# The first 500 steps of all engines in a listed order, and the first feed-forward unit in two halves

## The chip, the cores and the metric

The kernel runs on one core of one Trainium2 chip. The metric is the device time of one execution in microseconds, as the median of several runs.

The engines are named as in the profile: PE (TensorE; PEld are its weight loads), DVE (VectorE), ACT (ScalarE), POOL (GpSimd) and SP (SyncE, which issues nearly all DMAs).

## The reference

Two blocks follow one another. The first is a linear attention with decay, over 4 batches, 8 heads, 768 positions and 64 columns per head, in blocks of 64 positions:

```python
for b in range(nb):
    intra = np.einsum('bhic,bhjc->bhij', qb, kb) * Dmask[None]
    intra = np.einsum('bhij,bhjd->bhid', intra, vb)
    inter = np.einsum('bhid,bhde->bhie', qb * lam_pow[None], kv_state)
    out[:, :, sl] = intra + inter
    kb_dec = kb * rev_pow[None]
    kv_state = lam_block[None, :, None, None] * kv_state + np.einsum('bhsd,bhse->bhde', kb_dec, vb)
```

Its result, as 3072 rows of 512, goes through a feed-forward block with a leaky ReLU:

```python
h = x @ w_in                  # 512 x 2048, stored as 64-bit floats
g = np.maximum(0.01 * h, h)
out = (g @ w_out)             # 2048 x 512, stored as 64-bit floats
```

## The kernel before, in words

**Tiles.** The 3072 rows are 24 chunks of 128 rows (two blocks of 64); six chunks make a batch, and four chunks make a group `g` of 512 rows, six groups in all. The 2048 columns of `w_in` are eight pieces `p` of 256 columns. Group by piece is a *unit*, written (g,p): `up(g, p)` multiplies the group's 512 rows by the piece, applies the leaky ReLU and stores the result G in DRAM; `down` reads it back for the second product.

**Three products for one.** Operands are split into a high part h and a low part l, with a mixed part m of both, so that a unit has three products (h, l, m) for each of two halves `f` of the piece's columns. A product is four matmuls with 512 columns, one after the other into one PSUM bank (L640). After h and l ACT scales the bank in place (L658); after m ACT applies the ReLU into `gs` (L661), and SP stores `gs` (L664).

**A chunk of attention.** SP loads k and q (L338, two DMAs each) and v (L388). `transposes(c)` turns k and q on PE (L403), k into a bank and q into `pt`; ACT copies them out (L414, L415); k is scaled by the decay (L419) and q by its powers (L423). `scores(c)` multiplies q and k into the lower half of `psc` and k and v into the state's increments in its upper half (L313, 32 small matmuls each). DVE masks the scores (L452) and adds the increments to the state (L457, L459), with POOL multiplying the state by the decay in between (L462). `outputs(c)` sums masked scores by v and state by q into `po` (L313: 40 or 48 small matmuls, then, after a tiny read of `po` by DVE or ACT (L491), 8 or 16 more). ACT and DVE split the result into xh (L507), xl (L508) and xm (L510), the rows of the units' right-hand side.

**A piece of weights.** `w_in(p)` loads two halves of 512 KB into one of three buffers `raw` (L566), assembles 32-bit floats from the 64-bit words with three ACT steps (L578, L580, L582) and two DVE steps (L584, L585) per half, and splits them into wh (L591 on ACT or L593 on DVE), wl (L596) and wm (L602).

**Order.** The engines' instructions are not scheduled by the framework. Every step is given to a `Plan` by `add`, with the engines that may run it, its estimated length, what it reads and writes, and a rank from its place in the list `seq`. `emit` then simulates the engines with these lengths and the handover times `LAG`, always takes the step that can start first (by rank where several can), and issues the instructions in that order. Each engine runs its own steps strictly in order and waits by semaphores. `begin` and `end` bind a round's PE steps into a chain. Where the planned PE waits over 0.4 us before the first unit, `emit` puts in fillers: transposes of the identity without use (L266); nine more stand at the very start.

`seq` opens with chunks 0 to 3 one by one (`alone`), weight 1, chunk 4's start (`begun`), round 4, unit (0,1), weight 0, round 5, weights 2 and 3, units (0,0), (0,2), (0,3), round 6, and then unit (1,1) in two pieces of 384 and 128 rows, around round 7, weight 4, unit (0,4) and weight 7.

**Banks and buffers.** The units' banks are b10 and b2 for the first two, then b10, b11, b2 in turn. Transposes of k for chunks 0 to 3 use b11, those of q use `pt`. k, q and v of a chunk lie in one of two places by the chunk's parity.

Of the kernel before, what the change touches and what calls it, by code (L numbers as in the profile page):

```python
# [35 lines left out]

class Plan:
# [5 lines left out]
    SOON = dict(LAG, DMA=2.0)  # L43

    def __init__(self):
        self.ops, self.last, self.rank = [], {}, 0.0
        self.chain, self.chains = None, {}
        self.warm, self.slack, self.more = 0.0, 0.0, {}
        self.first = {"PE": 0.0, "ACT": 0.0, "DVE": 3.4, "POOL": 0.0, "DMA": 0.2}
        self.cold, self.idle, self.spare = 6.0, None, None  # L50
# [10 lines left out]
    def add(self, eng, us, fn, reads=(), writes=(), rank=0.0):  # L61

        n, deps = len(self.ops), set()
        for k in reads:
            w, r = self.last.setdefault(k, [None, []])
            if w is not None:
                deps.add(w)
            r.append(n)
        for k in writes:
            w, r = self.last.setdefault(k, [None, []])  # L70
            if w is not None:
                deps.add(w)
            deps.update(r)
            self.last[k] = [n, []]
        deps.discard(n)
        ways = {eng: us} if isinstance(eng, str) else dict(zip(eng, us))
        if self.slack:
            self.more[n] = self.slack
        if self.chain is not None:
            self.chains[self.chain].append(n)  # L80
        self.ops.append((ways, fn, deps, (self.rank + rank, n), set(writes)))

    def emit(self):
        n = len(self.ops)
        follows, heads = {}, {}
        for c in self.chains.values():
            m = [i for i in c if "PE" in self.ops[i][0]]
            for i in c[1:]:
                self.ops[m[0]][2].update(self.ops[i][2] - set(c))
            heads[m[0]] = m[1:]  # L90
            follows.update((i, m[0]) for i in m[1:])
        locked = []
        left = [len(o[2]) for o in self.ops]
        users = [[] for _ in range(n)]
        for i, o in enumerate(self.ops):
            for d in o[2]:
                users[d].append(i)
# [3 lines left out]
        for i, o in enumerate(self.ops):  # L101
            if not left[i]:
                for e in o[0]:
                    able[e].add(i)

        def since(i, e):
            return max((t + (0.0 if e == x != "DMA" else self.LAG[x]) for t, x in ends[i]), default=0.0)
# [6 lines left out]
        while len(done) < n:  # L114
            best = None
            for e in free:
                for i in able[e]:
# [3 lines left out]
                    if (best is None or (t, self.ops[i][3]) < best[:2]) and good(i, e, t):  # L121
                        best = (t, self.ops[i][3], i, e)
            t, _, i, e = best
            ways, fn = self.ops[i][:2]
# [4 lines left out]
            for x in ways:  # L129
                able[x].discard(i)  # L130
            us = ways[e]
            if e == "PE" and t < self.cold:
                us *= 1.5
            elif e == "DVE" and fn is not None and free["POOL"] > t:
                us += 0.4 * min(free["POOL"] - t, us)
            free[e] = t + us
            done.append((t, len(done), i, e))
            for u in users[i]:
                ends[u].append((free[e] + self.more.get(i, 0.0), e))
                left[u] -= 1  # L140
                if not left[u]:
                    for x in self.ops[u][0]:
                        able[x].add(u)
        self.timeline = sorted(done)
# [4 lines left out]
        for t, _, i, e in self.timeline:  # L149
            ways, fn, deps = self.ops[i][:3]  # L150
            t = max([soon[e]] + [over[d][0] + (0.0 if over[d][1] == e != "DMA" else self.SOON[over[d][1]]) for d in deps])
            if e == "PE":
                if self.spare in self.ops[i][4]:
                    self.idle = None
                if self.idle is not None and t > soon[e] + 0.4:
                    self.idle(int((t - soon[e] - 0.2) / 0.22))
            soon[e] = t + ways[e]
            over[i] = (soon[e], e)
# [4 lines left out]
def kernel(  # L163
# [25 lines left out]
    KT, EARLY = "b11", 2  # L189
    QS = 4  # L190
    KM = 2
# [29 lines left out]
    bank = {"b10": b1[0], "b11": b1[1], "b2": b2}  # L221
# [41 lines left out]
    def busy(n):  # L263

        for _ in range(n):
            nc.tensor.transpose(out=b1[0][:, 0:P], in_=ident, identity=ident)  # L266

    busy(WARM)
    nc.gpsimd.memset(zero, 0.0)
    plan = Plan()  # L270
    plan.idle, plan.spare, plan.warm = busy, "b10", 1.3 + 0.22 * WARM
# [7 lines left out]
    def move(us, fn, reads, writes, issue=0.5, rank=0.0, slack=SLACK):  # L279

        plan.slack = slack if steady else EARLY_SLACK
        if steady and not rank:
            rank = FIRST
        add("DMA", length(us, issue), fn, reads, writes, rank=rank)
# [3 lines left out]
    def factors_k():  # L288
        for i in range(2):
            nc.vector.tensor_copy(lam_h[:, i * HP:(i + 1) * HP], lam_b[:, i::2])  # L290
        nc.vector.tensor_tensor(eye, ident[:, 0:C2], ident[:, C2:C], op=ALU.add)
# [15 lines left out]
    add("DVE", 1.95, factors_k, [], ["fk", "sc"])  # L307
    add("DVE", 1.25, factors_q, [], ["fq"])
# [20 lines left out]
    pu = [psc[:, t, upper, :] for t in range(2)]  # L329

    def load_kq(c):
        b, n, i = of(c)
        for src, x, nm in ((k, 0, "k"), (q, 1, "q")):
            y, dst = src[b, :, n * C:(n + 1) * C, :], kqv[x][i]
# [4 lines left out]
            if nm == "k" or c < DV:  # L339
                move(1.15, go, [], [f"{nm}{i}"], issue=1.0)  # L340

    def run(c):

        lo = max(DV, c - c % TURN)
        return lo, c - c % TURN + TURN - lo

    def subs(first, n):
# [5 lines left out]
        ks = [(*rows(raw[-2], 0, 2), [f"raw{NRAW - 2}"]), (*rows(raw[-1], 2, 4), [f"raw{NRAW - 1}"])]  # L353
        qs = [(*rows(kqv_f[1], 0, HP), ["q0", "q1"])]

        if first == DV:
            ks = [(*rows(raw[0], 0, HP), ["raw0"])]
        elif first < DV + TURN:
            qs = [(*rows(w32f, 0, 2), ["w320", "w321"])] + [
                (*rows(lows[i].bitcast(F32), 2 + i, 3 + i), [f"low{i}"]) for i in range(2)]  # L360
# [25 lines left out]
    def load_v(c):  # L386
        b, n, i = of(c)
        move(1.15, lambda: nc.sync.dma_start(out=kqv[2][i], in_=v[b, :, n * C:(n + 1) * C, :].rearrange("h p d -> p h d")),  # L388
            [], [f"v{i}"])

    def transposes(c):
        b, n, i = of(c)
        tk, tq = kqv[0][i], kqv[1][i]
        if c < GC:
            z, key = bank[KT].rearrange("p (y t) -> p y t", y=HP), KT
            at = [z[:, y, :] for y in range(HP)]
        else:
            z, key = po[:, :, upper, :], "po"
            at = [po[:, y // 2, HP + y % 2 * 2:HP + y % 2 * 2 + 2, :].rearrange("p a t -> p (a t)") for y in range(HP)]
# [4 lines left out]

        if c < DV:
            add("PE", 0.44, lambda: go(tk, at), [f"k{i}"], [key])
            add("PE", 0.44, lambda: go(tq, [pt[:, y, :] for y in range(HP)]), [f"q{i}"], ["pt"])

        def copies():
            kT = kTs[i]  # L410
            into = kT if c < GC else kT.rearrange("p (t a) x -> p t (a x)", t=2)
            src = z if c < GC else z.rearrange("p t a x -> p t (a x)")
            if c < DV:
                add("ACT", 0.6, lambda: nc.scalar.copy(into, src), [key], [f"kT{i}"])  # L414
                add("ACT", 0.6, lambda: nc.scalar.copy(qTs[i], pt), ["pt"], [f"qT{i}"])  # L415
            kr = tk.rearrange("p (y x) d -> p y x d", x=2)
            nr = slice(0, C2 if n == NCB - 1 else P)
            add(*((("DVE", "POOL"), (0.7, 1.1)) if c < KM else ("POOL", 1.1)),
                lambda e="POOL": ENG[e].tensor_tensor(kr[nr], kr[nr], _bc(pow_k, 3, D)[nr], op=ALU.mult), ["fk"], [f"k{i}"])  # L419
# [404 lines left out]
```

## Time and profile before

| | us |
|---|---|
| median of three runs (610.5, 610.82, 612.51) | 610.82 |
| the profiled execution | 610.55 |
| its span, first to last instruction | 608.8 |
| PE busy (98% of the span) | 598.1 |
| DVE, ACT, POOL busy | 313.4, 269.1, 86.2 |
| start of the first transposes of the problem (chunk 0's k) | 3.99 |
| start of the first product of unit (0,1) | 28.84 |

The profile is of one execution, with times from the first instruction. A row of the timeline gives start, duration, engine, line, operation and tiles; in brackets it gives the engine's idle time just before and what ended it. Matmuls overlap in the pipeline, so the distance between two starts tells more of their cost than a duration does. Groups give busy time, the mean of one in nanoseconds, and the idle time ahead of them. The granted clock is a share of full speed.

### The profile page before, as it was taken

Reading aid. Unit: us, or ns where it says so; the run is one execution under the profiler, and the core shown is the slowest. Engines: PE = TensorE matmul, PEld = TensorE weight load, DVE = VectorE, ACT = ScalarE, POOL = GpSimd, SP = SyncE. Lnnn points to the kernel's source line nnn. Section 1 sums busy time; section 2 is a strip of 40 time slices with the busy share of each in tenths; the row PEclk is TensorE's granted clock in tenths of the full one; section 3 lists DMA queues with packets and bytes.
Section 4 is the critical chain, followed back from the end, with each engine's and each line's share of the span. In section 5 each row is a group of like instructions: output and inputs, shape, how many; then the busy total and the mean of one; then the engine's idle time right before and its main releaser. Section 6 shows DMA issues by size and latency. Waiting matters only on the chain.

```text
span 608.8 us, 12931 instructions
## 1 busy us (share of the span) xinstructions
PE 598.1 (98%) x5386; PEld 495.0 (81%) x5386; DVE 313.4 (51%) x418; ACT 269.1 (44%) x430; POOL 86.2 (14%) x90
## 2 busy tenths in 40 slices
PE   7799999999999999999999999999999999999997
PEld 6678888888888878888788888888888888888886
DVE  5899764334243426326366755545454554635531
ACT  4678974434455646555577522222222313214111
POOL 1654412105133004104000000000000000000000
PEclk9999999999999999999999999999999999999999
DMA  9999774667888878786686843524333333433201
GB/s 209 235 261 272 210 202 122 175 149 187 200 208 239 214 229 207 212 253 216 228 300 219 288 145 103 173 69 139 138 104 129 114 136 106 139 104 122 86 1 69
DMA packets 147754, 105.18 MB, mean 173 GB/s; under 512 B 123632, under 2 KB 124400, under 8 KB 147696
## 3 DMA queue, kind: packets, MB, share of 16 engines
q1 hardware_dynamic: 147408, 104.29, 58.6%
q8 instruction: 42, 0.69, 0.5%
q14 instruction: 16, 0.13, 0.1%
q10 hardware_dynamic: 288, 0.07, 0.0%
HBM read 68.69 MB, written 35.65 MB: 171 GB/s over the span
## 4 chain that ended last, share of the span: by engine, by line
PE 94%; DMA 2%; DVE 2%; ACT 1%; issue 0%; DVEq 0%; SPq 0%; ACTq 0%
PE b L640 42%; PE b L700 18%; PE po L700 11%; PE psc L700 11%; PE po L313 4%; PE psc L313 4%; PE pt L700 4%; DMA g<-gs 1%; DMA att<-in_v_dram 1%; PE pt L403 1%; DMA att<-in_k_dram 1%; PE po L403 0%; DVE wm L602 0%; ACT att L415 0%; DVE wl L596 0%; ACT gs L661 0%
## 5 line engine op out<-in xcount | busy, mean ns | idle before, releaser
L682 ACT ACTIVATE xh<-att 128x1024 fp32r<-128x1024 f32 x48 | 50.7, 1060 | 148.7 <-PE b L700 140.7
L683 DVE SCALAR_TENSOR_TENSOR xl<-att,xh 128x1024 fp32r<-128x1024 f32 x48 | 58.6, 1223 | 98.0 <-ACT xh L682 98.0
L640 PE MATMUL b<-xm,wm 128*128 128x512 f32 (+2 forms) x392 | 104.5, 392 | 0.3 <-ACT b L658 0.3
L640 PE MATMUL b<-xh,wh 128*128 128x512 f32 (+2 forms) x392 | 103.5, 387 | 0.8 <-ACT xh L507 0.8
L640 PE MATMUL b<-xl,wl 128*128 128x512 f32 (+2 forms) x392 | 103.3, 387 | 0.0
L640 PEld LDWEIGHTS b<-xh,wh 128*128 128x128 f32 x392 | 72.8, 188 | 16.5 <-ACT xh L507 0.9
L640 PEld LDWEIGHTS b<-xl,wl 128*128 128x128 f32 x392 | 72.7, 188 | 14.9 <-DVE wl L596 0.2
L640 PEld LDWEIGHTS b<-xm,wm 128*128 128x128 f32 x392 | 71.4, 188 | 15.6 <-ACT b L658 0.8
L658 ACT ACTIVATE b<-b 128x512 f32<-128x512 f32 (+2 forms) x97 | 55.9, 579 | 58.9 <-PE b L640 58.7
L661 ACT ACTIVATE gs<-b 128x512 f32<-128x512 f32 (+2 forms) x97 | 56.9, 592 | 44.5 <-PE b L640 37.9
L700 PE MATMUL b<-wh,xh 128*128 128x512 f32 x192 | 74.7, 389 | 0.0
L700 PE MATMUL b<-wl,xl 128*128 128x512 f32 x192 | 74.7, 389 | 0.0
L685 DVE SCALAR_TENSOR_TENSOR xm<-xl,xh 128x1024 fp32r<-128x1024 f32 x48 | 58.7, 1225 | 4.7
L462 POOL TENSOR_TENSOR att<-att 128x256 f32<-128x256 f32 x40 | 35.0, 874 | 57.6 <-DVE att L459 57.6
L700 PEld LDWEIGHTS b<-wl,xl 128*128 128x128 f32 x192 | 36.0, 187 | 7.5
L700 PEld LDWEIGHTS b<-wh,xh 128*128 128x128 f32 x192 | 36.1, 188 | 7.4
L452 DVE TENSOR_TENSOR att<-psc,att 128x512 f32<-128x512 f32 x24 | 16.5, 689 | 42.1 <-PE psc L313 42.0
L423 POOL TENSOR_TENSOR att<-att 128x512 f32<-128x512 f32 (+1 forms) x20 | 24.6, 1228 | 95.7 <-DVE att L383 46.8
L700 PE MATMUL psc<-wm,xm 128*128 128x512 f32 (+1 forms) x100 | 37.9, 384 | 0.0
L700 PE MATMUL psc<-wh,xh 128*128 128x512 f32 x96 | 37.3, 389 | 0.0
L700 PE MATMUL psc<-wl,xl 128*128 128x512 f32 x96 | 37.3, 389 | 0.0
L700 PE MATMUL po<-wh,xh 128*128 128x512 f32 x96 | 37.3, 389 | 0.0
(73 smaller groups left out, 784.9 us busy)
## 6 DMA issues: line engine op xcount, KB each, us to landing
att<-g SPq DMA_DIRECT2D x48, 512.0 KB, 3.2
g<-gs SPq DMA_DIRECT2D x47, 512.0 KB, 4.0
raw<-in_moe_w_in_dram SPq DMA_DIRECT2D x16, 512.0 KB, 5.1
raw<-in_moe_w_out_dram SPq DMA_DIRECT2D x16, 512.0 KB, 4.8
att<-in_k_dram SPq DMA_DIRECT2D x48, 128.0 KB, 4.1
att<-in_v_dram SPq DMA_DIRECT2D x24, 256.0 KB, 4.5
out_dram<-gs SPq DMA_DIRECT2D x23, 256.0 KB, 2.2
wo<-w SPq DMA_DIRECT2D x8, 512.0 KB, 5.7
```

Of the source, the lines that this page charges most:

```text
L313: nc.tensor.matmul(dst[HALF[cols]], lhsT=lhsT[HALF[rows]], rhs=rhs[HALF[rows]], start=start, stop=True, skip_group_check=True)
L403: nc.tensor.transpose(out=at[y], in_=src[:, 2 * y:2 * y + 2, :].rearrange("p a d -> p (a d)"), identity=ident)
L423: add(eng, us, lambda: e.tensor_tensor(o, x, _bc(pow_q, 2, 2)[:, :, m, :], op=ALU.mult), ["fq", dep], [f"qsT{i}"])
L452: add("DVE", 0.69, lambda: nc.vector.tensor_tensor(sc, psc[:, :, lower, :], decay, op=ALU.mult), ["psc", "fk"], ["sc"])
L462: add("POOL", 0.7, lambda new=new, j=j: nc.gpsimd.tensor_tensor(state[(j + 1) % 4], new, _bc(lam_c, 2, D), op=ALU.mult), [f"st{j % 4}", "f ...
L640: nc.tensor.matmul(dst, lhsT=w[z][:, kk * 2 * P + f * P:kk * 2 * P + (f + 1) * P], rhs=x[z][:, kk, toks], start=start and kk == 0, stop=kk ...
L658: add("ACT", ns, lambda b=b: nc.scalar.activation(out=b, in_=b, func=AF.Copy, bias=0.0, scale=S + 1.0), [], [kb], rank=-1.5)
L661: add("ACT", ns, lambda b=b, r=r: nc.scalar.activation(out=r, in_=b, func=AF.Prelu, bias=0.0, scale=1.0 / WS, alpha=0.01), [kb], [f"gs{jg} ...
L682: add("ACT", 1.05, lambda: nc.scalar.activation(out=h, in_=graw[j], func=AF.Copy, bias=0.0, scale=NEAR), reads, wr("h"))
L683: add("DVE", 1.25, lambda: nc.vector.scalar_tensor_tensor(l, graw[j], 1.0, h.bitcast(F32), op0=ALU.mult, op1=ALU.subtract), reads + [f"rh{ ...
L685: add("DVE", 1.25, lambda: nc.vector.scalar_tensor_tensor(m, l.bitcast(F32), -S, h.bitcast(F32), op0=ALU.mult, op1=ALU.add), [f"rh{j}", f" ...
L700: nc.tensor.matmul((to if z == 2 else acc[tb][0])[:, cols], lhsT=ring[j][z][:, f * T + tb * P:f * T + (tb + 1) * P], rhs=W[pp][z][:, f * d ...
```

## The change

The opening is no longer planned at build time. A constant `ORDER` holds 500 entries (step, engine) in which the opening's steps are issued; a negative entry stands for that many fillers (16 in all, after the nine at the start). The remaining steps are planned as before, from where the list ends.

- Unit (0,1) is cut into two halves of 256 rows (chunks 0 and 1, chunks 2 and 3), each with 256-column products of both `f` in one bank. Unit (1,1) is whole and comes after weight 7.
- k, q and v of chunks 2 and 3 get places of their own: in the two `gs` buffers, behind the q buffers and in the third `raw` buffer.
- Four banks (`pt`, b11, b10, b2) are shared by transposes, units, fillers and, for chunks 0 to 3, the state's increments, which leave `psc`; which bank a step gets is the one unused for longest. `raw`, `low` and `gs` buffers are chosen in the same way.
- The q scaling of chunks 4 to 7 moves from POOL to DVE (`QS`); the k scaling of chunks 2 to 7 may run on DVE or POOL (`KM`). In the list DVE scales k of chunks 1, 2, 4 and 5, POOL of 0, 3, 6 and 7.
- Estimated lengths, handover times and the rule for DVE steps beside POOL steps are altered in the planner.

The list's opening, by the names of the steps (T transposes, kv and go state and score matmuls, own, in0, in1 the output matmuls, Hf, Lf, Mf the products of a unit's part; a number is the chunk, or weight and half):

```
PE  6 fillers, Tk0 Tq0 kv0 go0, 1, own0 in0 Tk1 in1 kv1 Tq1, 1, go1 Tk2 own1 in0, 1, Tq2, 2, kv2 in1(1) Tk3 go2 Tq3
    H0(0,1)a own2 in0, 2, in1 L0a, 1, kv3 go3 H1a L1a own3 in0 Tq4 in1 M0a Tq5, 1, H0(0,1)b Tk4 L0b M1a kv4 go4 Tk5 ...
SP  k0 q0 v0 w1.1 k1 v1 q1 k2 w1.0 q2 v2 k3 q3 v3 w0.1 w0.0 q5 q4 k4 k5 v4 w2.1 w2.0 q6 k6 v5 ...
```

The core of the diff:

```diff
     def emit(self):
         n = len(self.ops)
+        listed = {i for i, _ in self.order if i >= 0}
+        deps = self.resolve([i for i, _ in self.order if i >= 0] + [i for i in range(n) if i not in listed])
...
+        for i, e in self.order:
+            if i < 0:
+                done.append((free[e], len(done), i, e))
+                free[e] -= 0.11 * i
+                continue
+            take(max(free[e], since(i, e)), i, e)
+        while len(done) < n + len(self.order) - len(listed):
...
-    KT, EARLY = "b11", 2
-    QS = 4
-    KM = 2
+    APART = 4
+    QS = 8
+    KM = 8
...
-    bank = {"b10": b1[0], "b11": b1[1], "b2": b2}
+    bank = {"pt": pt.rearrange("p y t -> p (y t)"), "b11": b1[1], "b10": b1[0], "b2": b2}
...
+    ORDER = [(3, "DMA"), (4, "DMA"), (-6, "PE"), (6, "PE"), (8, "ACT"), (7, "PE"), (5, "DMA"), (9, "ACT"), (0, "DVE"), 
...
+    spots = {x: z for x, z in {("k", 2): gs[0][:, 0, :], ("v", 2): gs[0][:, 1, :], ("q", 2): kqv_f[1][:, 2 * HP * C:3 * HP * C],
+             ("k", 3): gs[1][:, 0, :], ("v", 3): gs[1][:, 1, :], ("q", 3): raw[-1][:, :HP * C]}.items() if x[0] != "q" or x[1] // 2 not in PAIRS["q"]}
...
+        apart = c < APART
+        kp = [Slot("bank") for _ in range(n_pu)] if apart else ["psc"] * n_pu
...
-            kb = ("b10", "b2")[n_b % 2] if n_b < 0 else ("b10", "b11", "b2")[n_b % 3]
+            kb = Slot("bank")
...
-    seq = [("a", 0), ("a", 1), ("a", 2), ("a", 3), ("wi", 1), ("b", 4), ("r", 4), ("up", 0, 1), ("wi", 0), ("r", 5),
-           ("wi", 2), ("wi", 3), ("up", 0, 0), ("up", 0, 2), ("up", 0, 3), ("r", 6), ("up", 1, 1, 0, 3), ("r", 7),
-           ("wi", 4), ("up", 0, 4), ("wi", 7), ("up", 1, 1, 3, 4), ("up", 1, 3), ("up", 0, 7), ("up", 1, 2),
+    seq = [("a", 0), ("a", 1), ("a", 2), ("a", 3), ("wi", 1), ("b", 4), ("r", 4), ("up", 0, 1, 0, 2), ("up", 0, 1, 2, 4), ("wi", 0), ("r", 5),
+           ("wi", 2), ("wi", 3), ("up", 0, 0), ("up", 0, 2), ("up", 0, 3), ("r", 6), ("r", 7),
+           ("wi", 4), ("up", 0, 4), ("wi", 7), ("up", 1, 1), ("up", 1, 3), ("up", 0, 7), ("up", 1, 2),
```

## The prediction

> **What bounds the kernel now.** I read the busy line of the page, then what TensorE (PE) waits for, then the table of five-microsecond stretches, then PE's timeline where that table shows gaps.
>
> ```profile
> PE 598.1 (98%) x5386; PEld 495.0 (81%) x5386; DVE 313.4 (51%) x418; ACT 269.1 (44%) x430; POOL 86.2 (14%) x90
> ```
>
> PE is the bound: 598.1 of 608.8 us. From about 32 us it hardly waits, so the end can only move if PE becomes dense earlier, or if the matmuls of the problem take less PE time.
>
> ```profile
> PE psc L313 <- DVE att L459: 1.8, 2, 1.1
> PE psc L313 <- DMA att<-in_v_dram: 1.4, 1, 1.4
> PE b L266 <- POOL att L269: 1.4, 1, 1.4
> PE b L640 <- ACT xh L507: 0.8, 1, 0.8
> PE po L403 <- DVE xl L508: 0.5, 1, 0.5
> ```
> ```profile
> 20.00:25.00 5.00, 3.57 (x131) 2.77 (x132) 3.93 (x7) 3.34 (x6) 4.18 (x4) 1.00 1.00 263
> 25.00:30.00 5.00, 4.11 (x98) 3.17 (x90) 4.66 (x6) 3.22 (x6) 2.67 (x4) 1.00 0.87 226
> 30.00:35.00 5.00, 4.54 (x68) 3.47 (x70) 4.80 (x7) 4.04 (x7) 2.93 (x3) 1.00 1.03 240
> 35.00:40.00 5.00, 5.00 (x51) 3.86 (x44) 4.45 (x7) 2.96 (x7) 2.91 (x3) 1.00 0.95 305
> ```
>
> Columns: stretch, its length, busy time of PE, weight loads, VectorE (DVE), ScalarE (ACT), GpSimd (POOL), clock, DMA share, GB/s. PE is full from 35 us; before that DVE and the DMA are nearly full too, so the opening is limited by several things at once.
>
> ```profile
> 24.13 1.16 PE L313 MATMUL psc<-att 64*64 64x64 f32 x64 [1.41 <-DMA att<-in_v_dram]
> 25.22 0.76 PE L266 MATMUL b<-att 128*128 128x128 f32 x5
> 26.09 0.93 PE L313 MATMUL po<-att 64*64 64x64 f32 x48
> ...
> 28.84 2.11 PE L640 MATMUL b<-xh,wh 128*128 128x512 f32 x8 [0.78 <-ACT xh L507]
> 31.42 0.66 PE L403 MATMUL po<-att 128*128 128x128 f32 x4 [0.46 <-DVE xl L508]
> ```
>
> Chunk 3's score and state matmuls (24.13) stand behind its v; five fillers (L266, 0.76 us of useless PE work) bridge the wait for the masked scores; the first feed-forward product waits 0.78 us, because a whole unit needs chunk 3's xh; the next transposes wait 0.46 us for its xl.
>
> **A ledger.** I call lost time the clock minus the PE work of the problem done so far, each matmul at its dense start-to-start distance: 0.2275 us at 512 columns, 0.175 at 384, 0.11 for a transpose, 0.93 us per 64 score and state matmuls, 1.09 us per 64 output matmuls (rows from 50 us on). In the trace it is 14.4 us at 25, 17.6 at 35 and 18.5 at 45.
>
> **Following the list.** I decoded the 500 entries into steps and followed them: a step starts when its engine is free and its last input is there. Lengths are those of the trace: DVE 0.69, 0.42 and 1.22 us, the next queued step starting 0.08 before the end (20.60, 21.20); ACT 0.59 to 1.06, 0.11 before; POOL 1.06 and 0.62; small PE work of the first four chunks 15% slower than dense (64 score and state matmuls take 1.09 us at 13.13); 0.1 to 0.25 us for a handover; loads as they land before 33 us (256 KB of k, q or v about 1.15 us apart, 512 KB of weights 2.0). Before's own order, followed by these rules, must give its trace:
>
> ```
> lost time, us, at     10    15    20    25    30    35    45
> before, trace        7.5   9.8  12.0  14.4  16.7  17.6  18.5
> before, followed     7.6   9.8  11.9  14.0  16.8  17.5  19.0
> change, followed     7.5  10.0  12.4  14.4  15.2  15.6  16.6
> ```
>
> **The change part by part.**
>
> *First unit in halves.* Tokens of chunks 0 and 1 alone feed six products of 256 columns, about 2.9 us of work (six times four matmuls at 0.121, below). The list puts one in front of chunk 2's outputs and three around chunk 3's scores. They fill what before lost between 25 and 35 us: fillers 0.76, xh 0.78, xl 0.46, together 2.0 us. The table agrees: 3.2 us lost there before, 1.2 after: **-2.0**.
>
> *Own places for chunks 2 and 3, and the load order.* k, q and v of both wait for no buffer. But the second half of weight 1 goes third, before k of chunk 1, which lands at 10.2 instead of 8.1 us; v of chunk 3 lands at 21.8 instead of 24.0. By 25 us the two are worth nothing together (14.4 against 14.4): **0**. SP issues in the listed order, so a result's store (G) and the weight loads behind it wait for one another; in the following no PE step after 40 us waits for that.
>
> *Steps moved from POOL to DVE.* DVE gets three more k scalings (0.67) and four more q scalings (2.5 in all), some 4.5 us by 60 us. Its cover is that DVE steps overlapped by POOL's are stretched now:
>
> ```profile
> L585 DVE CUSTOM_DVE_ANT_0 w<-w,low 128x1024 uint16<-128x1024 uint16 x11 | 10.4, 943 | 0.9
> L584 DVE TENSOR_SCALAR w<-w 128x512 int32<-128x512 int32 x11 | 7.6, 688 | 0.6 <-ACT w L578 0.6
> L602 DVE SCALAR_TENSOR_TENSOR wm<-wl,wh 128x1024 fp32r<-128x1024 f32 x5 | 6.9, 1371 | 0.0
> ```
>
> These are groups by form from 15 to 70 us; undisturbed they take 690, 420 and 1220 ns, so 11 x 0.25 + 11 x 0.27 + 5 x 0.15 = 6.5 us is stretch. With less on POOL I expect most of the 4.5 us to come out of it. Between 35 and 45 us the table shows 1.0 us lost against before's 0.9: **+0.1**. If the cover fails, PE waits (rival below). [...]
>
> *Fillers.* The list has 16 (its negative entries), before ran 21 after the first nine. Those that fill a wait cost nothing; the five that count are in the 2.0.
>
> *Unit (1,1) whole.* Before it runs as 384 and 128 columns:
>
> ```profile
> 63.62 0.86 PE L640 MATMUL b<-xh,wh 128*128 128x384 f32 x4
> 64.32 0.85 PE L640 MATMUL b<-xl,wl 128*128 128x384 f32 x4
> ...
> 75.48 0.56 PE L640 MATMUL b<-xh,wh 128*128 128x128 f32 x4
> 75.88 0.61 PE L640 MATMUL b<-xl,wl 128*128 128x128 f32 x4
> ```
>
> Four start 0.70 us apart at 384 columns and about 0.41 at 128, so 0.175 + 0.104 = 0.279 per pair, against 0.2275 whole. Twenty-four pairs: **-1.2**. The halves of unit (0,1) go the other way. No 256-column matmul is in the trace; from 512 to 384 the distance falls by 0.0525, which gives 0.121 at 256, and the line between 128 and 384 gives 0.139. A pair costs 0.242 to 0.278 against 0.2275, so +0.4 to +1.2; I take **+0.4**, since the 384-column row is the nearer in kind (at 128 columns something else than the columns sets 0.104).
>
> *Four banks, new planning constants, everything after the list.* After 110 us PE waited 0.3 us for a bank step, so the gain is at most that. The rest is planned as before with slightly shorter steps; DVE is 13.09 of 20 us busy from 80 to 100 us, so PE has cover: **0**, with 1 us either way.
>
> **Sum:** -2.0 + 0.1 - 1.2 + 0.4 = -2.7 us. The profiled execution took 610.55 us (span 608.8), so 607.85; it lies 0.27 below the median of the three runs, 610.82, so I forecast a median of **608.1 us**. A measurement of this kernel can tell about 0.3% (1.8 us) from no change; the forecast is 0.45%.
>
> **Rivals.**
>
> *The gain is half eaten (609.0 to 610.5, no change that can be told).* Followed with quicker loads (512 KB in 1.85 us), before would be dense sooner too, and the difference at 45 us shrinks from 1.9 to 0.5 us; with the split's 0.8 that leaves 1.3, so 609.5. For it: the load distances are one run's. Against: by them before's own lost time at 45 us would be 16.4, and its trace has 18.5.
>
> *VectorE and ScalarE become the bound, slower (about 612.6).* The list makes PE dense earlier with less in stock, and fixes the order of all engines, so one late DVE step holds all behind it (masked scores, xl, then PE's transposes). Following both orders with handovers 0.2 us longer, PE waits in the change before chunk 5's states, unit (0,2)'s second product and chunk 8's transposes, and ends 2.6 us of lost time above before's: +2.6 - 0.8 = +1.8, a median of 612.6. The turning point is a handover 0.1 us longer, or DVE steps some 8% longer than undisturbed. For it: DVE is busy 4.66 to 4.80 us of five from 25 us on, and ACT would be about 90% busy from 32 to 62. Against: before, followed with undisturbed lengths, stays within 0.6 us of its trace from 10 to 70 us.
>
> *The clock falls (about 612).* The granted clock is 1.00 in every stretch, through waits of 1.41 us; the first fillers still run at 0.24 us each against 0.13 later. Were PE slow again for the third chunk, half of its work hidden in waits, some 4 us of small work would cost 1.5 to 4 us more. [...]
>
> *The change does nothing at the front* (the list is a planner's order again) is ruled out by the halves, which before does not run.
>
> **Numbers.** Forecast 0.60, half eaten 0.17, VectorE and ScalarE 0.17, clock 0.03, and 0.03 for more gain than the sum (the 1.2 us still lost from 25 to 35 us). The forecast's own spread, 1.5 us either way, reaches 609.6, so part of it counts as no change. Faster by over 0.3% 0.58, within 0.19, slower 0.23. The range runs from 605.9 (all of the 2.0 and half as much again, from 1 us after the list) to 612.2 (most of the VectorE rival).
>
> **What would show it.** Right: 256-column products between 21 and 32 us; PE without waits of over 0.5 us after 32 us; lost time near 15.6 at 35 us; no 384-column rows. Wrong: PE waiting on DVE or ACT lines between 35 and 65 us, DVE full there, or waits after 100 us.

## The result and the profile after

The median is 608.52 us (seven runs, 607.35 to 609.83) against 610.82 us before (seven runs, 610.5 to 612.51). The ratio is 0.9961, with a 95% interval of 0.9948 to 0.9974. The profiled execution took 607.92 us, its span 606.1 us. One execution each of two kernels below (997.68 us of the change again, 997.03 of weight 1.1 later) ran at a granted clock of 0.56, and one of the kernel before took 2108.93 us; they are left out of medians and ratios.

The total is close to the 608.1 us of the prediction, but its parts are not. The ledger of the prediction (lost time is the clock minus the dense PE work of the problem done so far; here a piece counts by its columns, 256 at 0.114 us, and a pair of 384 and 128 as one of 512, so that the price of cutting is in the lost time) shows where the gain is:

```
lost time, us, at          25    35    45   100   200   300   600
before                   14.4  17.6  18.5  21.3  23.2  26.7  25.5
change, forecast         14.4  15.6  16.6
change                   15.0  17.8  18.5  19.6  21.6  24.1  23.1
change, second profile   14.8  17.1  18.5  19.4  22.0  24.5  23.3
```

To 45 us nothing is gained. From 45 to 100 us 1.8 us are (2.8 lost before, 1.2 of it the price of the 384- and 128-column pieces, and 1.1 now; the list ends in that stretch), from 200 to 300 us another 1.0 us (3.5 against 2.5), and nothing elsewhere.

The busy line of the page after:

```profile
PE 595.4 (98%) x5381; PEld 494.4 (82%) x5381; DVE 308.5 (51%) x425; ACT 266.9 (44%) x428; POOL 73.4 (12%) x83
```

POOL is 12.8 us less busy, and DVE, which took the moved steps over, is not busier: its weight steps are stretched less.

What PE waits for, over the whole run (total, times, longest):

```profile
PE b L349 <- POOL att L352: 1.4, 1, 1.4
PE b L546 <- DMA gs<-in_k_dram: 1.3, 1, 1.3
PE b L410 <- DMA att<-in_v_dram: 1.1, 1, 1.1
PE psc L410 <- issue: 0.8, 1, 0.8
PE po L410 <- DVE att L637: 0.8, 2, 0.5
```

The first is the start. The waits on xh (0.8) and xl (0.5) that the first whole unit had before are gone. In their place stand loads (k of chunk 3, v of chunk 0) and 0.8 us of "issue", a stop for nothing that the profile names.

The stretches of the opening (stretch, length, busy PE, PEld, DVE, ACT, POOL, clock, DMA share, GB/s):

```profile
20.00:25.00 5.00, 3.95 (x110) 3.27 (x111) 4.59 (x8) 3.07 (x7) 2.58 (x3) 1.00 0.89 257
25.00:30.00 5.00, 4.15 (x127) 3.58 (x127) 3.74 (x7) 3.61 (x8) 0.66 (x2) 1.00 0.93 200
30.00:35.00 5.00, 5.00 (x109) 4.48 (x107) 4.85 (x10) 4.33 (x8) 0.74 (x1) 1.00 1.02 296
```

PE is full from 30 us instead of 35. From 25 to 30 us it is only 4.15 us busy, although DVE then has 1.3 us free and ACT 1.4: by the busy times no engine is the limit there, and the DMA is 0.93 full. PE's timeline shows the place:

```profile
21.05 0.44 PE L546 MATMUL b<-att,gs 128*128 128x128 f32 x2 [1.30 <-DMA gs<-in_k_dram]
...
24.72 0.74 PE L853 MATMUL pt<-xl,wl 128*128 128x256 f32 x4
25.30 0.27 PE L349 MATMUL b<-att 128*128 128x128 f32 x1
25.50 0.69 PE L410 MATMUL b<-gs 64*64 64x64 f32 x32
26.02 0.40 PE L410 MATMUL psc<-att 64*64 64x64 f32 x12
27.27 0.56 PE L410 MATMUL psc<-att 64*64 64x64 f32 x20 [0.85 <-issue]
27.76 0.74 PE L853 MATMUL pt<-xh,wh 128*128 128x256 f32 x4
```

PE stops inside one step: after 12 of the 32 matmuls of chunk 3's scores (go3), which wait for nothing between them.

### The profile page after: what moved, and what is told of

Same layout as the page of the kernel before. It is cut to its first block, busy times and chain, and to the rows that moved or that the text cites. A ratio compares the mean times of both kernels' runs of the same rounds, so it can differ in the third digit from the quotient of the medians.

```text
span 606.1 us, 12896 instructions
## 1 busy us (share of the span) xinstructions
PE 595.4 (98%) x5381; PEld 494.4 (82%) x5381; DVE 308.5 (51%) x425; ACT 266.9 (44%) x428; POOL 73.4 (12%) x83
## 4 chain that ended last, share of the span: by engine, by line
PE 96%; SPq 2%; DMA 1%; issue 0%; DVE 0%; DVEq 0%; ACT 0%
PE b L853 33%; PE b L920 18%; PE pt L853 11%; PE po L920 11%; PE psc L920 11%; PE po L410 4%; PE pt L920 4%; PE psc L410 3%; SPq L466 2%; DMA gs<-in_k_dram 1%; PE b L546 1%; PE po L546 0%; SPq L781 0%; SPq L524 0%; PE pt L546 0%
## 5 line engine op out<-in xcount | busy, mean ns | idle before, releaser
L853 PE MATMUL b<-xm,wm 128*128 128x512 f32 (+1 forms) x292 | 77.6, 391 | 0.0
L853 PE MATMUL b<-xh,wh 128*128 128x512 f32 (+1 forms) x292 | 77.4, 389 | 0.0
L853 PE MATMUL b<-xl,wl 128*128 128x512 f32 (+1 forms) x292 | 77.4, 388 | 0.0
L853 PEld LDWEIGHTS b<-xl,wl 128*128 128x128 f32 x292 | 54.2, 188 | 11.2
L853 PEld LDWEIGHTS b<-xh,wh 128*128 128x128 f32 x292 | 54.0, 188 | 11.1
L853 PEld LDWEIGHTS b<-xm,wm 128*128 128x128 f32 x292 | 53.5, 188 | 11.4 <-ACT b L878 0.3
L878 ACT ACTIVATE b<-b 128x512 f32<-128x512 f32 x72 | 42.0, 586 | 34.8 <-PE b L853 34.8
L881 ACT ACTIVATE gs<-b 128x512 f32<-128x512 f32 x72 | 42.6, 597 | 30.3 <-PE b L853 24.3
L647 POOL TENSOR_TENSOR att<-att 128x256 f32<-128x256 f32 x40 | 30.9, 772 | 86.8 <-DVE att L644 73.9
L799 DVE TENSOR_SCALAR w<-w 128x512 int32<-128x512 int32 x32 | 14.9, 468 | 44.1 <-ACT w L793 44.0
```

Of the source, the lines that this page charges most:

```text
L647: add("POOL", 0.62, lambda new=new, j=j: nc.gpsimd.tensor_tensor(state[(j + 1) % 4], new, _bc(lam_c, 2, D), op=ALU.mult), [f"st{j % 4}", " ...
L799: add("DVE", 0.42, lambda: nc.vector.tensor_scalar(d, d, 3, None, op0=ALU.logical_shift_left), [], [key], lock=True)
L853: nc.tensor.matmul(dst, lhsT=w[z][:, kk * 2 * P + f * P:kk * 2 * P + (f + 1) * P], rhs=x[z][:, kk, toks], start=start and kk == 0, stop=kk ...
L878: add("ACT", ns, lambda b=b: nc.scalar.activation(out=b(), in_=b(), func=AF.Copy, bias=0.0, scale=S + 1.0), [], [kb], rank=-1.5)
L881: add("ACT", ns, lambda b=b, r=r: nc.scalar.activation(out=r(), in_=b(), func=AF.Prelu, bias=0.0, scale=1.0 / WS, alpha=0.01), [kb], [kg], ...
```

## The experiments

Theory 1 is the prediction's sum: the halves fill gaps of the opening (-2.0 + 0.4), unit (1,1) whole gives -1.2. Theory 2 is what the ledger says at first sight: the opening gives nothing, unit (1,1) gives -1.8. Theory 3, from the first four kernels: the parts are worth something only in the list's order. All runs, with the ratio to the kernel before on the same chip, lost time, and the stop of issue near 26 us in the profiled execution:

```
kernel                        median   ratio, 95% interval       lost at 45  at 100  stop
change, again                 609.01   0.9961 [0.9947, 0.9976]   18.5        19.4    -
before, (1,1) whole           611.98   1.0008 [0.9995, 1.0022]   19.2        22.3    -
change, (1,1) split           610.19   0.9989 [0.9975, 1.0003]   19.8        23.4    1.95
change, (0,1) whole           617.56   1.0091 [1.0069, 1.0113]   24.5        26.0    1.85
change, planner's order       616.04   1.0073 [1.0057, 1.0088]   22.6        26.2    0.49
before, (0,1) in halves       614.92   1.0067 [1.0047, 1.0087]   19.2        24.1    -
change, no listed fillers     609.16   0.9968 [0.9956, 0.9980]   20.4        21.5    2.41
change, two products earlier  610.58   0.9991 [0.9974, 1.0008]   18.6        19.9    0.46
change, no own places         609.58   0.9975 [0.9960, 0.9989]   18.1        19.6    -
change, weight 1.1 later      608.89   0.9967 [0.9954, 0.9981]   18.8        19.9    1.92
change, weight 0.0 later      612.20   1.0019 [1.0007, 1.0031]   21.2        22.3    0.35
change, lighter loads         606.89   0.9934 [0.9918, 0.9950]   16.9        17.8    -
```

### The change again

No edit.

> The changed kernel as it is, run again beside the variants. Theory 1 (the prediction's sum) and theory 2 (the opening gave nothing; unit (1,1) whole and something after 200 us gave it all) both expect 608.5 us within 0.6 and a lost time of 18.5 us at 45 us by the ledger. What it tells: whether the PE gaps of the opening (1.30 us on k3 at 19.7 us, 1.1 us on v0 at 6.5 us, 0.85 us of issue at 26.4 us) stand in a second profile. If the gap of issue is an accident of one execution, it moves or is gone, and lost time at 45 us falls by up to 0.85 us; if it is fixed by the program, it stands at the same instruction.

609.01 us, lost time 18.5 us at 45 us. Of the stop of issue 0.19 us is left in this profile (at the same record), yet the opening ends where it did: PE waits for loads instead.

```profile
PE b L410 <- DMA gs<-in_v_dram: 0.4, 1, 0.4
...
PE po L546 <- DMA att<-in_k_dram: 0.4, 1, 0.4
...
PE psc L410 <- DMA att<-in_v_dram: 0.3, 1, 0.3
```

The first is v of chunk 2 at 18.6 us; the last two are k of chunk 6 (the expectation of the last experiment calls it k7) at 38.3 and v of chunk 4 at 32.9 us.

### Unit (1,1) whole, alone, in the kernel before

```diff
-           ... ("r", 6), ("up", 1, 1, 0, 3), ("r", 7), ... ("wi", 7), ("up", 1, 1, 3, 4), ("up", 1, 3), ...
+           ... ("r", 6), ("r", 7), ... ("wi", 7), ("up", 1, 1), ("up", 1, 3), ...
```

> The kernel before with one part of the change alone: unit (1,1) is made whole (its 384 and 128 columns are planned as one unit of 512), everything else is planned as before. Theory 1 priced this part at -1.2 us: 610.8 - 1.2 = 609.6 us, lost time at 100 us by the ledger 21.3 - 1.2 = 20.1 us. Theory 2 reads -1.8 us in the trace of after between 45 and 100 us and puts all of it to this part: 609.0 us, lost time 19.5 us at 100 us; and the loss of 3.5 us between 200 and 300 us (23.2 to 26.7) stays.

Neither theory held: 611.98 us, no gain. PE now waits once, at 64 us, for a weight's high part:

```profile
62.37 2.12 PE L640 MATMUL b<-xm,wm 128*128 128x512 f32 x8
66.18 2.11 PE L640 MATMUL b<-xh,wh 128*128 128x512 f32 x8 [1.69 <-ACT wh L591]
```

Before, the 384-column piece of unit (1,1) was the work that PE had for that moment: it runs from 63.62 us, while ACT makes that high part (L591, from 64.38 us). The split was a bridge, paid with 1.2 us; whole, the unit needs an order in which the weight is ready sooner. A second thing follows: with before's three banks this kernel loses 2.5 us from 200 to 300 us (25.7 to 28.2), as the change does with four. The 1.0 us that the change gains there is therefore not the fourth bank's.

### Unit (1,1) split, in the change

Unit (1,1) is cut into 384 and 128 columns again; the first piece takes the listed places of the whole unit, the second's eight products stand behind the products of chunk 8.

> The changed kernel with this one part undone: unit (1,1) again as 384 and 128 columns, the eight pieces of 128 columns put into the list behind the products of chunk 8; everything else as in the changed kernel. Theory 1: +1.2 us, 609.7 us. Theory 2: +1.2 to +1.8 us between 45 and 100 us by the ledger and nothing later, 609.7 to 610.3 us; the lost time between 200 and 300 us stays at 2.5 us (21.6 to 24.1).

610.19 us, 1.2 us more than the change on the same chip, at the low end of both expectations. In the trace 45 to 100 us costs 2.5 us more: 24 x 0.0515 = 1.24 us for the pieces, 0.9 us in two waits (0.41 and 0.48 by the distance of starts) that my places for the second piece make, and 0.4 us that I did not trace. The opening has its own loss here, a stop of issue of 1.95 us.

### Unit (0,1) whole, in the change

The products of the first half leave the list; those at 512 columns stand from where the second half stood, the second `f` behind the first.

> The changed kernel with the first unit (0,1) whole again in the list: its first products, at 512 columns, stand where the second half stood (from about 32 us), and the gaps before them get no products. Theory 1 gives the halves -2.0 us of filled gaps and +0.4 us for their 256-column products: without them 608.5 + 1.6 = 610.1 us, lost time at 45 us 20.1 us. Theory 2 gives the halves nothing but what the 256-column products cost, since what they fill is made up of waits for loads and for instructions that stay: 608.5 us within 0.3, lost time at 45 us within 0.3 us of 18.5.

617.56 us, far more than either said. The whole unit's two banks are held longer and no work is left for the waits, so that chunk 5 and chunk 6 come late (waits of 1.52 us on ACT ahead of 36.5 us and 2.14 us on DVE ahead of 44.0 us). This is the price of a list in which a hole was torn, more than the worth of the halves; it shows that they are no ornament of this order, and not that they are worth 8.5 us.

### The planner's order with everything else of the change

```diff
-    ORDER = [(3, "DMA"), (4, "DMA"), (-6, "PE"), ...]
+    ORDER = []
```

> The changed kernel with an empty list: the greedy planner orders all of it, with the halves of (0,1), unit (1,1) whole, the own places and the four banks kept. Theory 1 and theory 2 both put the order of the first 500 at about nothing of its own (608.5 within 1). Theory 3 (from the two variants run so far: whole (1,1) in the planner's order made PE wait 2.08 us on weights at 64 us, and without its halves the list opens 6 us worse): neither the halves nor unit (1,1) whole is worth anything alone; the list is what keeps the weights ahead of unit (1,1) and the halves in their gaps. Then the planner's order loses: 610.5 to 614 us.

### The halves alone, in the kernel before

```diff
-           ... ("r", 4), ("up", 0, 1), ("wi", 0), ...
+           ... ("r", 4), ("up", 0, 1, 0, 2), ("up", 0, 1, 2, 4), ("wi", 0), ...
```

> The kernel before with one part of the change alone: the first unit (0,1) in two halves, all of it in the planner's order. Theory 1: the halves are free to fill gaps of 25 to 35 us, -2.0 + 0.4: 609.2 us, lost time at 45 us 17 us by the ledger. Theory 3: the planner's rank keeps the halves behind the chunks and their weights, so that the gaps of the opening stay: 610.8 to 611.2 us (the 256-column products cost 16 x 0.005 x 2 = +0.2 us), lost time at 45 us 18.3 to 19.

616.04 and 614.92 us: the direction of theory 3, but 2.0 and 3.7 us above its ranges. The halves, the places and the banks in the planner's order lose 4.7 us to before by the medians, the halves alone 3.6 us. In the latter the opening is level with before to 40 us (18.0); the loss comes from 40 us on: a load of k at 41 us (0.9 us by the distance of starts), and a stop of 1.35 us at 55.8 us, again "issue". Neither of the two parts tried alone is worth anything, nor are the parts without the list; the list without the parts was tried only with one of them undone at a time.

### Without the list's fillers

Negative entries leave the list (14 fillers before go3 is done).

> The changed kernel without the list's 15 fillers (transposes of the identity that keep TensorE busy, about 0.2 us each). Theory 1 put the fillers at 0: they stand in gaps. With them gone the granted clock could fall in the opening. If they lie in gaps whose end another engine or a load sets, the time stays at 608.5 within 0.5; if TensorE's clock falls below 0.9 for a stretch of 3 us or more before 30 us, up to +1.7 us (3.4 us at half speed). On the gap of issue at 26 us: in three of four executions of this list TensorE stopped at the same record, number 475, for 0.85 to 1.95 us, until 2.4 to 2.75 us after a transfer of 16 KB of instructions began. If the gap is tied to the count of instructions, it again comes near record 475, which is 14 records later in the work (the last of the 32 output-state products of chunk 3); if it is tied to the work itself (a semaphore, a bank), it stays at the same product of chunk 3.

609.16 us: the fillers (16 by the list's negative entries, not 15) are worth nothing that can be told in the median. The profiled execution is the slowest of eleven (610.45 us) and the only one with a clock below 0.999. What this run decides is the stop. Before it now come 26 of go3's 32 matmuls instead of 12:

```profile
24.56 0.63 PE L410 MATMUL psc<-att 64*64 64x64 f32 x26
27.59 0.34 PE L410 MATMUL psc<-att 64*64 64x64 f32 x6 [2.41 <-issue]
```

Fourteen records fewer, and the stop comes fourteen matmuls later in the work: it stands at the same count, record 474 of PE. Behind the stop, the clock falls (columns: stretch, length, busy PE, clock, DMA share, GB/s):

```profile
24.00:28.00 4.00, 1.59 (x66) 1.00 0.91 202
28.00:30.00 2.00, 2.00 (x44) 0.72 0.92 208
30.00:33.00 3.00, 3.00 (x50) 0.62 0.99 273
33.00:36.00 3.00, 3.00 (x67) 1.00 0.71 209
```

### Two products ahead of chunk 3's scores

In the list H and L of the second `f` of the first half move from behind go3 to ahead of kv3.

> The changed kernel with one move in the list: the eight 256-column products (H and L of the second f of the first half) stand ahead of chunk 3's state and score products instead of behind them. If the gap of issue near 26 us is a wait for instructions tied to record 475, it comes eight records earlier in the 64-column burst and is shorter by about 8 x 0.12 = 0.9 us (0 to 1.0 us instead of 0.85 to 1.95), but what those products covered, the mask of chunk 3 on VectorE ahead of own3, is then open for 0.5 to 0.9 us: 608.5 us within 0.6, and less spread. If the gap is tied to the work (chunk 3's products), it stays at the same product and comes 0.9 us later, and the time is 609.4 us.

```profile
26.64 0.28 PE L410 MATMUL psc<-att 64*64 64x64 f32 x4
27.39 0.68 PE L410 MATMUL psc<-att 64*64 64x64 f32 x28 [0.46 <-issue]
28.85 0.69 PE L410 MATMUL po<-att,gs 64*64 64x64 f32 x32 [0.78 <-DVE att L637]
```

Eight records more ahead of go3, and the stop comes after 4 of its matmuls instead of 12: the count again. It is shorter, and the wait on the mask (0.78 us) that the products covered is open, as expected. The median, 610.58 us, is worse than expected and its runs spread further (608.50 to 614.21). The record tells part of the reason: the four executions with a granted clock of 1.000 (the profiled one among them) took 608.50 to 609.53 us, the eight with 0.997 or 0.994 took 609.67 to 614.21. Over a span of 607 us 0.997 is a loss of 1.8 us, about one stretch of 3.41 us at half speed such as the traces of other runs show (last section), and 0.994 two. What makes the clock fall more often in this order, and the rest of the spread, stay open.

### Without own places for chunks 2 and 3

```diff
-    spots = {x: z for x, z in {("k", 2): gs[0][:, 0, :], ...}
+    spots = {}
```

> The changed kernel without the own places of chunks 2 and 3: their k, q and v go into the buffers of chunks 0 and 1 and wait until those are used; list and halves unchanged. The prediction put places and load order together at 0: 608.5 within 0.5. The rival: the places are worth what k2, k3 and v3 then land later (before's v3 landed at 24.0 instead of 22.6 us), 1.4 to 4 us: 610 to 612.5 us, lost time at 25 us 16.5 to 19. For the gap of issue at record 474: fewer loads are queued at 21 to 24 us, so if queued loads are what delays the 16 KB of instructions (request near record 355, start 2.1 to 3.6 us later in the list's kernels, 0.4 to 1.35 us later in the three with before's load order), the start comes within 0.4 to 1.5 us and the gap is gone.

609.58 us, between the two expectations; lost time 18.1 us at 45 us, although the clock of the profiled execution is at half speed from 13.15 to 19.98 us. The interval overlaps that of the change, so the 0 of the prediction for places is not refuted, though up to about 2 us cannot be ruled out by the times. The loads speak for 0: k and v of chunk 3 land at 19.6 and 22.1 us, no later than in the change (21.0 and 22.6). There is no stop in this profile.

### Weight 1's second half later

In SP's list w1.1 moves from ahead of k1 to behind q1, and one ACT step of it moves along.

> The changed kernel with one move in the load order: the second half of weight 1 is issued after q of chunk 1 instead of ahead of k of chunk 1 (its ScalarE step moves behind the copies of chunk 1). k1 lands about 1.6 us earlier (8.5 instead of 10.1 us), the weights of unit (0,1) about 2 us later. If the waits of chunk 1 (0.6 and 0.8 us at 11 to 14 us) are what costs, 607.5 to 608.0 us; if the halves then wait for the weights at 22 us, 609.5 us or more. The prediction's 0 for the load order says 608.5 within 0.5.

608.89 us, the same as the change: lost time at 25 us is 0.6 to 0.8 us less (14.2), and in the profiled execution a stop of 1.92 us takes it away:

```profile
24.83 0.40 PE L410 MATMUL psc<-att 64*64 64x64 f32 x12
27.15 0.56 PE L410 MATMUL psc<-att 64*64 64x64 f32 x20 [1.92 <-issue]
```

### Weight 0's first half later

> The changed kernel with one move in the load order: the first half of weight 0 (512 KB) is issued behind q5, q4, k4 and k5 instead of ahead of them. In the list's kernels 512 KB of weight are in flight when the instructions for record 474 are asked for (21 to 22.5 us). If queued loads delay them, their start comes about 1 us sooner only if what is queued then is less; q5 and q4 take its place, so by this theory the lag stays at 2 to 3.5 us and the gap at 0 to 2 us. The products of unit (0,0) wait for the weights from 33 us if these had no slack: w00 lands about 3 us later (28.5 instead of 25.4 us). 608.5 us within 0.6 if there are 3 us of slack, 610 to 611 if not.

612.20 us, ratio 1.0019 [1.0007, 1.0031]. In this order the kernel computes something else than the reference, for a reason that I did not find, so its time is no evidence. Its trace still counts for the stop, which is there: 0.35 us, after the same record 474. The packet of instructions begins 1.7 us after record 355, sooner than the 2 to 3.5 us that the theory of queued loads expected here.

### What the stop is

The page of the change lists 42 packets of 16 KB on a queue of kind "instruction":

```profile
q8 instruction: 42, 0.69, 0.5%
```

PE and its weight loads are 2 x 5381 = 10762 instructions, for which 42 packets make 64 bytes each, so I take them for PE's program. The packets' times against PE's records:

```
                           PE at record   fetch     PE runs on   stop
                           355            begins    (474)
before                     19.71          20.15     24.82        -
before, (1,1) whole        19.93          21.28     25.18        -
change                     22.43          24.83     27.27        0.85
change, again              21.62          23.73     25.87        -
change, (1,1) split        20.94          24.54     27.29        1.95
change, (0,1) whole        21.52          24.18     26.78        1.85
change, planner's order    20.36          22.06     24.40        0.49
before, (0,1) in halves    20.18          21.47     24.86        -
change, no listed fillers  21.90          25.05     27.59        2.41
change, two earlier        22.11          25.07     27.39        0.46
change, no own places      22.46          24.03     26.74        -
change, weight 1.1 later   21.23          24.59     27.15        1.92
change, weight 0.0 later   21.56          23.27     25.90        0.35
change, lighter loads      21.65          23.34     25.58        -
```

Wherever PE stops it runs on 2.3 to 2.8 us after the packet of 16 KB began, and where it reaches record 474 2.7 us or more after that, it does not stop. In between, at 2.06 to 2.24 us (weight 0.0 later, change again, lighter loads), the stop is short: 0.35, 0.19 and 0.09 us, the last two too short to be listed as a wait. The other stops on "issue" above 0.4 us fit the same count: the planner's order also stops after records 349 and 1240 (0.41 and 1.09 us), the halves alone after record 984, and each runs on 2.2 to 2.5 us after a packet of q8 began. From 349 to 476 are 127 matmuls, from 476 to 984 four times 127, from 984 to 1240 twice 128, and 10762 / 42 = 256 instructions a packet are 128 matmuls with their weight loads.

The list's denser opening takes PE from record 355 to 474 in 3.1 to 4.6 us (before: 5.1), and the packet begins later after record 355: 0.4, 1.3 and 1.4 us in the three kernels of before's order, 1.6 to 3.6 us in the list's and the change's. That record 355 is where it is asked for is my inference from this spacing of 127 or 128 matmuls a packet; no trace shows it. That queued loads hold the packet back is not shown: the delays without own places and with lighter loads are short (1.6 and 1.7 us), but with all loads the planner's order and weight 0.0 later have 1.7 us as well. The stop itself, its place by count and its end 2.3 to 2.8 us after a packet began are shown.

### Lighter loads

```diff
-            if kind == "wi":
+            if kind == "wi" and p in (0, 2, 3):
+                nc.sync.dma_start(out=r64[:, 256:], in_=w_in_r[:, 2 * h + 1, p * 2 * P:(p + 1) * 2 * P])
+            elif kind == "wi":
```

> The changed kernel with lighter loads: of the weight loads of the first products after unit (0,1) (weights 0, 2 and 3, six loads of 512 KB between 18 and 45 us) only half of the rows is loaded, so 1.5 MB less; every other step, its order and its length stay (the products run on what the buffer held before, so this kernel computes something else). It tells what took the place of the 2.0 us that the prediction expected from the opening. If the loads do (they keep the DMA 0.9 to 1.0 full from 10 to 45 us, and the waits for v4 and k7 at 33 and 38 us in the second profile of the changed kernel are theirs, as is the queue ahead of the instructions for record 474), lost time at 45 us falls from 18.5 to 16.5 to 17.2 us and the time to 606.5 to 607.5 us. If the chain of engine steps does, lost time at 45 us stays at 18.0 to 18.5 us and the time at 608.5 within 0.6.

606.89 us, ratio 0.9934 [0.9918, 0.9950], 0.27% or 1.6 us below the ratio of the change, whose interval it just touches; lost time at 45 us is 16.9 us, also 1.6 less. With 1.5 MB less to load PE is full from 20 us on:

```profile
20.00:25.00 5.00, 4.96 (x121) 3.97 (x125) 5.00 (x9) 4.05 (x8) 2.58 (x3) 1.00 1.06 274
25.00:30.00 5.00, 5.00 (x147) 4.47 (x148) 4.84 (x9) 4.47 (x9) 1.36 (x2) 1.00 0.82 181
```

The steps, their order and their engines are those of the change, and the opening now comes out almost as the prediction had followed it (16.6). So the chain of engine steps allows the gain, and the transfers take it: loads that land late, or PE's instructions. How much is due to each is not told apart: in the change it is k of chunk 3 and the stop, in its second profile almost only loads.

## Why the prediction was right, and where it was not

**The total** was right within 0.4 us: 608.1 forecast, 608.52 measured. That is luck: a term of -2.0 gave nothing, and two later stretches gave more than forecast (-1.8 against the -1.2 of unit (1,1), and -1.0 against 0 after the list).

**First unit in halves, -2.0: failed.** By the ledger 0.0 at 45 us in both profiles, 0.2 of it the price of 256 columns. The step that failed is not the filling itself: the waits on xh (0.78) and xl (0.46) went, and 256-column products run from 22.46 us on. It is the assumption "loads as they land before 33 us", smooth at 1.15 us per 256 KB and 2.0 us per weight half. In the change k of chunk 3 lands at 21.0 us, just as its transposes could start (wait 1.30), v of chunk 3 at 22.6 instead of 21.8, and PE's own instructions, which I did not count as a load at all, stop it for 0.85 us. So the prediction's own sign, a lost time of 15.6 us at 35 us, did not show (17.8 and 17.1). With lighter loads 1.6 us of the 2.0 are there. The rival "the gain is half eaten" had the size of the loss but another mechanism (quicker loads that help before).

**Halves at 256 columns, +0.4: in range.** The distance in the trace is 0.118 us (0.121 estimated), so 48 x 0.0043 = +0.2 us. What I did not price is that the first matmul after other work takes 0.20 to 0.22 us. Seven blocks begin that way, 0.6 us in all, though whole products have such starts too; so the term is +0.2 to +0.8.

**Unit (1,1) whole, -1.2: right in size, wrong in condition.** No 384-column product of a unit is left; splitting it again costs 1.2 us in the median. But alone, in the planner's order, it gives nothing (1.0008), because a wait of 1.69 us on a weight opens. The stretch from 45 to 100 us gained 1.8 us, the 1.2 and 0.6 more; I did not trace the 0.6.

**Steps moved from POOL to DVE, +0.1: right.** The cover held. The two stretched weight steps and the last one of each weight, by form from 15 to 70 us:

```profile
L800 DVE CUSTOM_DVE_ANT_0 w<-w,low 128x1024 uint16<-128x1024 uint16 x12 | 8.5, 718 | 0.8 <-ACT low L797 0.8
...
L817 DVE SCALAR_TENSOR_TENSOR wm<-wl,wh 128x1024 fp32r<-128x1024 f32 x5 | 6.1, 1212 | 0.0
L799 DVE TENSOR_SCALAR w<-w 128x512 int32<-128x512 int32 x12 | 5.8, 490 | 1.3 <-ACT w L793 1.2
```

They take 718, 1212 and 490 ns where they took 943, 1371 and 688: 12 x 0.225 + 5 x 0.159 + 12 x 0.198 = 5.9 us, more than the 4.5 us moved. That POOL's steps are what stretched them shows in before's whole trace: beside no POOL step the three take 691, 1223 and 424 ns on average, beside one 1049, 1371 and 761. L584, the last, reads one tile only and is stretched most (424 to 761 ns); why a POOL step stretches a DVE step no run shows. The +0.1 itself cannot be told from the loads: 35 to 45 us cost 0.7 and 1.4 us in the two profiles, against 1.0 forecast. The rival that DVE and ACT become the bound has nothing for it: PE's waits on them stay below 0.6 us each and lie ahead of 30 us, but for 0.3 us at 291 us.

**Own places, load order, fillers, 0: not refuted** (609.58, 608.89 and 609.16 us without them or with one load moved; each interval overlaps that of the change, which tells no more than about 2 us).

**After the list, 0: wrong by 1.0 us, inside the 1 us allowed.** Before loses 0.5 us ahead of 223.23 us, where it waits for a bank step on ACT (L658, 0.34 us idle and a slow restart), and a further 0.4 us at other starts of its 512-column products. Two kernels with its three banks and another order in the opening lose 2.5 us there too (the table of (1,1) whole, and the halves alone, 27.6 to 30.1). So it is not the number of banks; which detail of before's order it is stays open.

**The clock rival** was given 0.03, with before's clock of 1.00 through a wait of 1.41 us against it. In the two profiles of the change it did not act, but in the variants a stop of 1.95, 1.85 and 2.41 us was followed by a fall, and not every execution is free of it: one of the change's seven (609.83 us) has a granted clock of 0.994, and of the second measurement's eleven six have 0.994 or 0.997. So have eleven of 29 executions of the kernel before beside them (0.996 or 0.997). The difference is not made by it: the executions of that measurement at 0.999 or 1.000 alone have medians of 608.56 and 611.0 us. But the rival was nearer than I thought.

## What to carry to other kernels

Following a list step by step tells whether the engines allow a gain; whether the transfers do is another question, and it needs its own test, such as the same kernel with lighter loads. A split that looks like waste (384 + 128 columns) may be a bridge over a wait: before pricing its removal, look up what PE would do at that moment instead. When PE stops inside a run of small matmuls that wait for nothing, count its records and look at the instruction queue. When executions of one kernel spread, compare their granted clocks first.

## What was not expected of the hardware

- PE stopped for 0.35 to 2.41 us in eight profiles near 26 us, at about the same record (474; 475 and 476 in two), inside a burst of 64-column matmuls some 15 ns apart, and ran on 2.3 to 2.8 us after a packet of 16 KB on the queue of instructions began: by count and times it was out of instructions.
- The granted clock fell to half for 3.41 us after such a stop in three profiles (stops of 1.85, 1.95 and 2.41 us) and not in a fourth (1.92). One such stretch is what the table without fillers shows: 0.72 over 2 us and 0.62 over 3 us are 1.1 + 2.3 = 3.4 us at half speed. It also fell after waits of another kind: from 14.85 us in the planner's order (1.62 us for a load), from 34.12 us with weight 0.0 later (2.31 us for ACT), and from 13.15 us, for 6.83 us, without own places, where no wait after the first two microseconds exceeds 0.82 us. In the 3.41 us ahead of each fall PE was busy 0.34 to 0.63 of the time. The share alone does not decide: no fall followed the 1.92 us stop, where PE was busy 0.39 of the time from 24.00 us to the end of the stop at 27.15 us, nor in the change a stretch of 0.57 (6.68 to 10.10 us).
- SP took 3.00 us to issue one DMA (the first of q of chunk 1, at 5.91 us) where its neighbours take 0.51, with the loads of chunk 1 and a weight outstanding; all loads behind it in the list wait that long.
